# The first block's attention pair by pair of heads, and the first block six weight steps ahead of the second

## The chip, the cores and the metric

The kernel runs on one core of a Trainium2 chip. Its engines run side by side, each with its own instruction queue: TensorE (PE) multiplies, VectorE (DVE), ScalarE (ACT) and GpSimd (POOL) work elementwise, and SyncE (SP) issues most of the data transfers. The time is the device time of one execution in microseconds, and the figure compared is the median of several.

## The reference

Three layers follow each other: a linear attention, a dense feed-forward layer, and a layer with eight experts of which each token takes one.

```python
kv  = einsum('bhsd,bhse->bhde', k, v)          # 4 batches, 8 heads, 576 tokens, 64 columns
out = einsum('bhsd,bhde->bhse', q, kv)
x   = out / sqrt(mean(out*out, -1) + 1e-6) * g_norm      # then [2304, 512]
g   = maximum(x @ w_in, 0) ** 2                # w_in [512, 2048]
x   = g @ w_out                                # w_out [2048, 512]
e   = argmax(x @ w_gate);  gate = softmax(x @ w_gate)[e]  # 8 experts, capacity 576
out = gate * (maximum(x @ w1[e], 0) @ w2[e])   # w1[e] [512, 1024], w2[e] [1024, 512]
```

## The kernel before

**Blocks and units.** The 2304 tokens are six blocks of 384 (`BT`), each of three tiles of 128. A block goes through attention, then through the feed-forward layer, whose 2048 hidden columns are cut into 16 weight steps f of 128. One block at one step is a unit (j, f): `mm1` (L268) is the first product and its squared rectifier, `mm2` (L288) the second product, two units later (`LAG`). All products in full precision are split in a high and a low part and done in three passes (`PASSES`), so each operand needs both parts.

**Weights of the feed-forward layer.** A step's two matrices, w_in and w_out, arrive as 64-bit numbers (`load_m` L142, two transfers of 512 KB a step). `cvt_m` (L151) turns them into 32-bit numbers: ScalarE rescales the upper half (L168), VectorE masks (L169), shifts (L170) and merges (L174). `split_m` (L179) lets ScalarE cast the high part (L183) and GpSimd subtract the low part (L184). In the loop over units, unit (0, f) converts step f + 2 and loads step f + 3.

**Attention of a block.** Heads go in four pairs, so that two heads fill 128 rows. `kv` (L206) multiplies keys and values of one pair and copies the two diagonal blocks to `kvb`, one on ScalarE, one on VectorE. `attn_out` (L217) takes one tile of tokens through all four pairs; ScalarE squares (L236), VectorE sums (L238), GpSimd scales and takes the power -0.5 (L240, L242). `attn_mul` (L244) multiplies on VectorE, and `attn_tr` (L251) transposes on TensorE, with the high part scaled on ScalarE (L259) and the low part on VectorE (L260) into `xT`.

**Order of the work.** The loop over units at the end of the listing writes the program, but a scheduler that works with estimated costs reorders TensorE, VectorE, ScalarE and GpSimd inside a block marked `manual_schedule(engines={SP})`; only SP's queue stays as written. `LEAD = 4` (L525): the first four units are block 0 alone, then units of block 0 and block 1 alternate, so that one converted weight serves both. The second block's attention (`kv_pieces(1)`, `attn_pieces(1)`) is spread over units 0 to 3 (L647). Fills of the scratch and output arrays with zeros (`zeros`) are spread over the units between (1, 2) and (0, 15).

```python
for p in range(NPAIR): kv(0, p)              # L565
for t in range(TB):    attn_out(t)           # L567
for t in range(TB):    attn_mul(t); attn_tr(t)
for f in range(2):     cvt_m(f); split_m(f, wpool)
```

**Buffers.** The pool `wpool` has 24 places of 4 KB a partition. Keys, values and queries of the first two blocks, the staged weights and the split weights of the first 12 steps share them, so a load waits until an earlier tile of its place has been used. The products go to eight banks of PSUM, `pk`: units use pk[0] and pk[1], block 0's results pk[2] to pk[4], and the attention of the front the banks pk[5] to pk[7] in turn (`misc`).

Of the kernel before, what the change touches and what calls it, by code (L numbers as in the profile page):

```python
# [7 lines left out]
F32 = mybir.dt.float32  # L8
F32R = mybir.dt.float32r
# [10 lines left out]
P = 128  # L20
# [6 lines left out]
def attn_moe_kernel(ctx: ExitStack, tc: tile.TileContext, cap, kp, vp, qt, gn, wm, wg, wgt, w1, w2, ident, tri, out):  # L27
# [123 lines left out]
    def cvt_m(f):  # L151


        ws = [stg.pop(("m", f, i)).bitcast(I32).rearrange("p (n t) -> p n t", t=2) for i in range(2)]
        if f < 12:
            h = wpool2.tile([P, 2, 512], F32, tag="w", name="ch")
            o = wpool2.tile([P, 2, 512], F32, tag="w", name="cf")
            parts = [(h, o, slice(0, 2))]
            cvt[f] = [o[:, i, :] for i in range(2)]
        else:  # L160
            hs = [(apool1, apool)[i].tile([P, 1, 512], F32, tag="qx"[i], name="ch") for i in range(2)]
            os = [(apool, apool1)[i].tile([P, 1, 512], F32, tag="kv"[i], name="cf") for i in range(2)]
            parts = [(hs[i], os[i], slice(i, i + 1)) for i in range(2)]
            cvt[f] = [o[:, 0, :] for o in os]
        for h, o, sl in parts:
            hi, oi = h.bitcast(I32), o.bitcast(I32)
            for n, w in enumerate(ws[sl]):
                nc.scalar.activation(out=h[:, n, :], in_=w[:, :, 1].bitcast(F32), func=AF.Copy, scale=2.0 ** -112)  # L168
            nc.vector.tensor_scalar(oi, hi, -(1 << 31), None, op0=ALU.bitwise_and)  # L169
            nc.vector.scalar_tensor_tensor(  # L170
                out=oi, in0=hi, scalar=3, in1=oi, op0=ALU.logical_shift_left, op1=ALU.bitwise_or
            )
            for n, w in enumerate(ws[sl]):
                nc.vector.scalar_tensor_tensor(  # L174
                    out=oi[:, n, :], in0=w[:, :, 0], scalar=29, in1=oi[:, n, :],
                    op0=ALU.logical_shift_right, op1=ALU.bitwise_or,
                )

    def split_m(f, pool):  # L179
        os = cvt.pop(f)  # L180
        for o, d in zip(os, (wi, wo)):
            w = d[f] = pool.tile([P, 2, 512], F32R, tag="w", name="w")
            nc.scalar.copy(w[:, 0, :], o)  # L183
# [22 lines left out]
    def kv(b, p):  # L206
        k, v = kt.pop((b, p)), vt.pop((b, p))
        ps = misc()
        for c in range(NCH):
            nc.tensor.matmul(ps[:, :P], lhsT=k[:, c, :], rhs=v[:, c, :], start=c == 0, stop=c == NCH - 1)  # L210
# [52 lines left out]
        )  # L263


    gt = {}

    def mm1(s):  # L268
        j, f = units[s]
        h = pk[s % 2][:, :BT]  # L270
        n = 0
        for c in range(KD):
            for a, m in PASSES:
                nc.tensor.matmul(  # L274
                    h, lhsT=wi[f][:, a, c * P:(c + 1) * P], rhs=xT[j][:, m, c, :],
                    start=n == 0, stop=n == 3 * KD - 1,
                )
# [244 lines left out]
        d[e, 2 * h], d[e, 2 * h + 1] = split_w(k, engs, pair_tiles(k))  # L522
        ahead(4)

    LAG, LEAD = 2, 4  # L525
    HOT = 9
    MIDDLE = 416
    units = []

    with tc.manual_schedule(engines={mybir.EngineType.SP}):  # L530

        cold = gpool.tile([P, BT], F32, tag="rr", name="cold", bufs=2)[:, :P]
        nc.vector.memset(cold, 0.0)
# [13 lines left out]
        for p in range(NPAIR):
            load_kv(0, p)
            if p == 0:
                nc.sync.dma_start(out=id_sb, in_=ident)  # L550
                nc.sync.dma_start(out=gn_sb, in_=gn)
# [6 lines left out]
        load_m(2)
        load_kv(1, 2)
        load_kv(1, 3)  # L560
        nc.sync.dma_start(out=wg_raw, in_=wg)
        nc.sync.dma_start(out=tri_sb, in_=tri)
        for t in range(TB, 2 * TB):
            load_q(t)
        for p in range(NPAIR):  # L565
            kv(0, p)
        for t in range(TB):  # L567
            attn_out(t)
        for t in range(TB):
            attn_mul(t)  # L570
            attn_tr(t)
        for f in range(2):
            cvt_m(f)
            split_m(f, wpool)
# [501 lines left out]
```

## Time and profile before

| | us |
|---|---|
| median of 3 runs | 759.19 (756.44 to 760.04) |
| the profiled execution | 755.1 |
| its span, first to last instruction | 753.2 |
| TensorE busy | 715.7 (95%) |
| VectorE busy | 371.6 (49%) |
| ScalarE busy | 309.5 (41%) |
| GpSimd busy | 292.3 (39%) |

The shares are means over stages that differ. By 40 slices of the span (18.8 us each), TensorE's busy tenths begin 6 6 7 8 and are then 9 (90% or more) until the last two; VectorE's begin 2 9 8 9 8 6 6. Matmuls are pipelined and their ends modelled. A weight load (PEld) runs beside the matmul before it. "Idle before" is time in which the engine had nothing running ahead of the instruction, with what ended it behind the arrow.

### The profile page before, as it was taken

The numbers are of one execution on the slowest core, as the hardware profiler recorded it, in microseconds if no ns is written. First come the engines' busy times: TensorE is split into PE (matmuls) and PEld (weight loads), VectorE is DVE, ScalarE is ACT, GpSimd is POOL, SyncE is SP. The second block draws the span as 40 slices with busy tenths as digits, with TensorE's granted clock in tenths as the row PEclk, the third lists the DMA queues.
The fourth block names the chain that finished last, engine by engine and source line by source line (L and its number), as shares of the span: only waits on it lengthen the run. The fifth ranks groups of instructions, "written<-read, shape, count | busy, mean of one in ns | idle before, by whom it ended". The sixth has DMA issues, their size and how long they took to land. (4 is left out here: it accounts for less than half of the span.)

```text
span 753.2 us, 12061 instructions
## 1 busy us (share of the span) xinstructions
PE 715.7 (95%) x4012; PEld 637.5 (85%) x4012; DVE 371.6 (49%) x833; ACT 309.5 (41%) x650; POOL 292.3 (39%) x288
## 2 busy tenths in 40 slices
PE   6678999999999999999999999999999999999985
PEld 6667999898899989989898988897888898889764
DVE  2989866548982594349634973331043221133011
ACT  2455454323222332233233264244276544376362
POOL 2566333112022200220130089043469746386881
PEclk9899999999999999999999999999999999999999
DMA  9946798401032202210010176043537554456530
GB/s 326 378 169 201 264 364 293 150 15 67 1 112 87 67 1 70 88 29 0 15 57 1 49 241 204 26 150 121 171 102 219 199 170 148 149 188 212 180 129 19
DMA packets 38016, 102.36 MB, mean 136 GB/s; under 512 B 4451, under 2 KB 4707, under 8 KB 37920
## 3 DMA queue, kind: packets, MB, share of 16 engines
q1 hardware_dynamic: 34912, 91.99, 36.4%
q0 software_dynamic: 3008, 9.10, 3.2%
q8 instruction: 59, 0.97, 0.5%
q14 instruction: 37, 0.30, 0.1%
HBM read 77.78 MB, written 23.91 MB: 135 GB/s over the span
## 5 line engine op out<-in xcount | busy, mean ns | idle before, releaser
L274 PE MATMUL pk<-xT,w 128*128 128x384 f32 x1152 | 223.1, 341 | 8.5 <-POOL w L184 4.6
L293 PE MATMUL pk<-w,g 128*128 128x512 f32 x864 | 218.4, 394 | 2.5 <-ACT g L285 2.5
L274 PEld LDWEIGHTS pk<-xT,w 128*128 128x128 f32 x1152 | 201.5, 188 | 18.6 <-POOL w L184 5.8
L195 POOL TENSOR_TENSOR w<-st,w 128x512 fp32r<-128x512 f32 x128 | 161.5, 1295 | 83.1 <-ACT w L191 83.0
L293 PEld LDWEIGHTS pk<-w,g 128*128 128x128 f32 x864 | 160.2, 188 | 31.7 <-ACT g L285 3.1
L282 ACT ACTIVATE rr<-pk 128x384 f32<-128x384 f32 x96 | 47.1, 492 | 153.6 <-PE pk L274 153.4
L817 PE MATMUL hb<-x,w 128*128 128x256 f32 (+2 forms) x672 | 96.7, 303 | 0.3
L817 PEld LDWEIGHTS hb<-x,w 128*128 128x128 f32 x672 | 93.8, 189 | 1.1 <-issue 0.2
L284 DVE TENSOR_TENSOR pk<-pk,rr 128x384 f32<-128x384 f32 x96 | 54.0, 563 | 74.6 <-ACT rr L282 73.7
L871 DVE SCALAR_TENSOR_TENSOR g<-hb,g 128x576 fp32r<-128x576 f32 (+3 forms) x72 | 40.5, 585 | 97.5 <-ACT g L870 96.5
L103 POOL DMA_INDIRECT disp<-y,sli x18 | 19.1, 1059 | 173.0 <-DVE sli L410 52.9
L355 DVE SCALAR_TENSOR_TENSOR junk<-y,wgb 128x512 f32<-128x512 f32 x120 | 78.0, 684 | 0.7 <-ACT y L313 0.6
L191 ACT CAST w<-st 128x512 fp32r<-128x512 f32 x128 | 71.7, 620 | 13.8 <-DMA st<-in_w 13.4
L285 ACT CAST g<-pk 128x384 fp32r<-128x384 f32 x96 | 46.0, 480 | 72.6 <-DVE pk L284 71.0
L286 DVE TENSOR_TENSOR g<-pk,g 128x384 fp32r<-128x384 f32 x96 | 53.3, 556 | 36.7 <-ACT g L285 36.0
L184 POOL TENSOR_TENSOR w<-cf,w 128x512 fp32r<-128x512 f32 x32 | 47.3, 1494 | 60.9 <-ACT w L183 56.3
L903 PE MATMUL hb<-w,g 128*128 128x512 f32 x264 | 65.7, 407 | 3.1 <-DVE g L871 2.5
L903 PEld LDWEIGHTS hb<-w,g 128*128 128x128 f32 x264 | 50.0, 193 | 15.7 <-DVE g L871 3.4
L870 ACT ACTIVATE g<-hb 128x576 fp32r (+3 forms) x72 | 34.9, 513 | 33.9 <-PE hb L817 29.2
L103 POOL DMA_INDIRECT out<-o,meta x22 | 21.3, 970 | 42.0 <-ACT o L911 17.8
L919 DVE SCALAR_TENSOR_TENSOR o<-bk,meta,o 64x512 f32<-64x512 f32 x3 | 2.3, 752 | 69.5 <-ACT o L918 51.0
L240 POOL TENSOR_SCALAR ms<-ss 128x8 f32<-128x8 f32 x18 | 4.6, 254 | 77.6 <-DVE ss L238 77.3
(138 smaller groups left out, 648.8 us busy)
## 6 DMA issues: line engine op xcount, KB each, us to landing
st<-in_w SPq DMA_DIRECT2D x64, 512.0 KB
st<-in_wm SPq DMA_DIRECT2D x32, 512.0 KB
disp<-zrow SPq DMA_DIRECT2D x9, 1028.0 KB
xr<-disp SPq DMA_DIRECT2D x32, 257.0 KB
k<-in_kp SPq DMA_DIRECT2D x16, 320.0 KB
v<-in_vp SPq DMA_DIRECT2D x16, 320.0 KB
q<-in_qt SPq DMA_DIRECT2D x18, 256.0 KB
out<-zrow SPq DMA_DIRECT2D x9, 512.0 KB
```

Source lines behind the costliest of these rows:

```text
L184: nc.gpsimd.tensor_tensor(w[:, 1, :], o, f32(w[:, 0, :]), op=ALU.subtract)
L191: nc.scalar.copy(w[:, 0, :], s[:, i, :])
L195: e.tensor_tensor(w[:, 1, :], s[:, i, :], f32(w[:, 0, :]), op=ALU.subtract)
L274: nc.tensor.matmul(h, lhsT=wi[f][:, a, c * P:(c + 1) * P], rhs=xT[j][:, m, c, :], start=n == 0, stop=n == 3 * KD - 1,)
L282: nc.scalar.activation(out=r, in_=h, func=AF.Relu)
L284: nc.vector.tensor_tensor(h, h, r, op=ALU.mult)
L285: nc.scalar.copy(g[:, 0, :], h)
L286: nc.vector.tensor_tensor(g[:, 1, :], h, f32(g[:, 0, :]), op=ALU.subtract)
L293: nc.tensor.matmul(ysets[j == 1][i], lhsT=g[:, a, i * P:(i + 1) * P], rhs=wo[f][:, m, :], start=f == 0 and n == 0, stop=f == NF - 1 and n ...
L355: nc.vector.scalar_tensor_tensor(out=junk, in0=yt[j * TB + i][:, :DM], scalar=1.0, in1=wgb[e // 2][:, e % 2, :], op0=ALU.mult, op1=ALU.mul ...
L817: nc.tensor.matmul(h, lhsT=w1_at(e, f // 2, a, c)[:, f % 2 * P:(f % 2 + 1) * P], rhs=x[:, m, c, o:o + w], start=k == 0, stop=k == 3 * KD - 1,)
L903: nc.tensor.matmul(ps[:k, :], lhsT=lhs(f, a), rhs=we2[e, f][:, b, :], start=n == 0, stop=n == len(passes) * NF2 - 1,)
```

## The change

The first block's attention is written pair by pair, and in a block in which no engine is reordered (`manual_schedule()`). Four new functions handle one pair for all three tiles: `first_out`, `first_red`, `first_mul`, `first_tr`, and `first_low` for the low part. They have 384 columns in place of 512, and use six banks in turn. The queries are loaded behind pair 0's keys. The conversion of step 0 is cut in two halves, one for each matrix, and stands among the last pairs; that of step 1 follows behind. `in_order` makes the conversions' rescaling wait for its turn behind the first block (`marks`), and the products of the second block's keys stand behind unit 2. `LEAD` goes from 4 to 6, and the second block's attention is spread over units 2 to 5. Its last two pairs of keys and its queries are loaded behind the weights of steps 3 and 4.

```diff
@@ cvt_m, split_m
-            parts = [(h, o, slice(0, 2))]
+            parts = [(h[:, a:a + n], o[:, a:a + n], slice(a, a + n)) for a, n in (((0, 1), (1, 1)) if f == 0 else ((0, 2),))]
...
+        return [lambda part=part: cvt_part(ws, *part) for part in parts]
+    def cvt_part(ws, h, o, sl):
+        for n, w in enumerate(ws[sl]):
+            a = nc.scalar.activation(out=h[:, n, :], in_=w[:, :, 1].bitcast(F32), func=AF.Copy, scale=2.0 ** -112)
+            if "cvt" in marks:
+                in_order(a, marks["cvt"])
...
@@ kv
+            if "kv" in marks:
+                in_order(a, marks["kv"])
...
+    def first_out(p):
+        ps = ops[p] = misc()
+        for t in range(TB):
+            nc.tensor.matmul(
+                ps[:, t * P:(t + 1) * P], lhsT=qtt[t][:, p, :], rhs=kvb[0][:, p, :],
+                start=t == 0, stop=t == TB - 1, skip_group_check=True,
+            )
...
+        nc.scalar.activation(out=x, in_=ps[:, :BT], func=AF.Square)
+    def first_red(p):
+        nc.vector.tensor_reduce(out=ss, in_=x.rearrange("p (h e) -> p h e", e=DH), axis=AX.X, op=ALU.add)
+        nc.gpsimd.tensor_scalar(ms, ss, 1.0 / DH, 1e-6, op0=ALU.mult, op1=ALU.add)
+        nc.gpsimd.tensor_tensor(r, ms, expo[:, :2 * TB], op=ALU.pow)
...
+    def first_tr(p):
+        for t in range(TB):
+            nc.tensor.transpose(ps[:, t * P:(t + 1) * P], x[:, t * P:(t + 1) * P], id_sb)
+        marks["first"] = nc.scalar.activation(out=d[:, 0, p, :], in_=ps[:, :BT], func=AF.Copy, scale=gn_sb)
...
@@ mm1
+        if s == 2:
+            marks["kv"] = a
...
-    LAG, LEAD = 2, 4
+    LAG, LEAD = 2, 6
-    with tc.manual_schedule(engines={mybir.EngineType.SP}):
+    with tc.manual_schedule():
...
+        load_kv(0, 0)
+        for t in range(TB):
+            load_q(t)
+        load_kv(0, 1)
+        load_kv(0, 2)
+        load_kv(0, 3)
+        load_m(0)
+        load_m(1)
+        load_m(2)
+        load_kv(1, 0)
+        load_kv(1, 1)
+        free[:] = pk[2:8]
+        kv(0, 0)
+        first_out(0)
+        first_red(0)
+        first_mul(0)
+        first_tr(0)
+        kv(0, 1)
+        first_low(0)
+        first_out(1)
+        first_red(1)
+        kv(0, 2)
+        first_out(2)
+        first_mul(1)
+        first_red(2)
+        first_tr(1)
+        kv(0, 3)
+        first_low(1)
+        first_out(3)
+        first_mul(2)
+        first_red(3)
+        first_tr(2)
+        first_low(2)
+        c_in, c_out = cvt_m(0)
+        c_in()
+        split_m(0, wpool, (0,))
+        first_mul(3)
+        first_tr(3)
+        first_low(3)
+        c_out()
+        split_m(0, wpool, (1,))
...
+    with tc.manual_schedule(engines={mybir.EngineType.SP}):
+        marks["cvt"] = marks["first"]
+        for c in cvt_m(1):
+            c()
+        split_m(1, wpool)
...
-        put(0, LEAD, kv_pieces(1) + attn_pieces(1))
+        put(2, LEAD - 2, kv_pieces(1) + attn_pieces(1))
...
+                if s == 0:
+                    load_kv(1, 2)
+                    load_kv(1, 3)
+                if s == 1:
+                    for t in range(TB, 2 * TB):
+                        load_q(t)
```

**TensorE, the front.** Before, from the first pair's product on (v, k are values and keys, kvb the diagonal blocks, q the queries, id_sb the transpositions):

```order
L210 MATMUL pk_93<-v,k 128x128 x5
L210 MATMUL pk_94<-v,k 128x128 x5
L210 MATMUL pk_95<-v,k 128x128 x5
L210 MATMUL pk_93<-v,k 128x128 x5
L228 MATMUL pk_94<-kvb_128,q 128x128 x4
L228 MATMUL pk_95<-kvb_128,q 128x128 x4
L228 MATMUL pk_93<-kvb_128,q 128x128 x4
L255 MATMUL pk_94<-id_sb,x 128x128 x4
L255 MATMUL pk_95<-id_sb,x 128x128 x4
L255 MATMUL pk_93<-id_sb,x 128x128 x4
L210 MATMUL pk_94<-v,k 128x128 x5
L210 MATMUL pk_95<-v,k 128x128 x5
```

Now, from the same place:

```order
L224 MATMUL pk_90<-v,k 128x128 x5
L286 MATMUL pk_91<-kvb_128,q 128x128 x3
L314 MATMUL pk_92<-id_sb,x 128x128 x3
L224 MATMUL pk_93<-v,k 128x128 x5
L286 MATMUL pk_94<-kvb_128,q 128x128 x3
L224 MATMUL pk_95<-v,k 128x128 x5
L286 MATMUL pk_90<-kvb_128,q 128x128 x3
L314 MATMUL pk_91<-id_sb,x 128x128 x3
L224 MATMUL pk_92<-v,k 128x128 x5
L286 MATMUL pk_93<-kvb_128,q 128x128 x3
L314 MATMUL pk_94<-id_sb,x 128x128 x3
L314 MATMUL pk_95<-id_sb,x 128x128 x3
```

A pair's outputs and transpositions now stand ahead of the next pair's product; the second block's keys (pk_94 in the last two rows before) are no longer here but behind the third unit.

**VectorE, the front.** Before, from the sums of the first block's rows on (ss the sums, cf the converted weights, ch their rescaled halves):

```order
L238 TENSOR_REDUCE ss<-x 128x8 x2
L246 TENSOR_TENSOR x<-pk_94,r 128x512
L238 TENSOR_REDUCE ss<-x 128x8
L246 TENSOR_TENSOR x<-pk_95,r 128x512
L169 TENSOR_SCALAR cf<-ch 128x1024
L260 SCALAR_TENSOR_TENSOR xT<-pk_94,gn_sb,xT 128x4x128
L260 SCALAR_TENSOR_TENSOR xT<-pk_95,gn_sb,xT 128x4x128
L246 TENSOR_TENSOR x<-pk_93,r 128x512
L170 SCALAR_TENSOR_TENSOR cf<-ch,cf 128x1024
L169 TENSOR_SCALAR cf<-ch 128x1024
L260 SCALAR_TENSOR_TENSOR xT<-pk_93,gn_sb,xT 128x4x128
L174 SCALAR_TENSOR_TENSOR cf<-st_176,cf 128x512
```

Now, from the last pairs on, with L183, L184 and L188 for the three steps of a conversion:

```order
L229 COPY kvb_128<-pk_92 64x64
L321 SCALAR_TENSOR_TENSOR xT<-pk_91,gn_sb,xT 128x384
L305 TENSOR_TENSOR x<-pk_90,r 128x384
L297 TENSOR_REDUCE ss<-x 128x6
L321 SCALAR_TENSOR_TENSOR xT<-pk_94,gn_sb,xT 128x384
L183 TENSOR_SCALAR cf<-ch 128x512
L184 SCALAR_TENSOR_TENSOR cf<-ch,cf 128x512
L188 SCALAR_TENSOR_TENSOR cf<-st_176,cf 128x512
L305 TENSOR_TENSOR x<-pk_93,r 128x384
L321 SCALAR_TENSOR_TENSOR xT<-pk_95,gn_sb,xT 128x384
L183 TENSOR_SCALAR cf<-ch 128x512
L184 SCALAR_TENSOR_TENSOR cf<-ch,cf 128x512
```

The first conversion, which stood among the first rows' scaling, now stands behind three of the four pairs and its second half behind all.

**ScalarE, between steps.** Before, around the rescaling of steps 5 and 6 (rr, g: a unit's first product; w: a cast weight):

```order
L282 ACTIVATE rr<-pk_89 128x384
L168 ACTIVATE ch<-st_456 128x512
L183 CAST w<-cf 128x512 x2
L168 ACTIVATE ch<-st_458 128x512
L285 CAST g<-pk_89 128x384
L259 ACTIVATE xT<-pk_93,gn_sb 128x4x128
L282 ACTIVATE rr<-pk_88 128x384
L168 ACTIVATE ch<-st_538 128x512
L168 ACTIVATE ch<-st_540 128x512
L183 CAST w<-cf 128x512 x2
```

Now, around the rescaling of steps 5 and 6:

```order
L180 ACTIVATE ch<-st_432 128x512
L347 CAST g<-pk_89 128x384
L197 CAST w<-cf 128x512 x2
L180 ACTIVATE ch<-st_434 128x512
L252 ACTIVATE x<-pk_94 128x512
L344 ACTIVATE rr<-pk_88 128x384
L180 ACTIVATE ch<-st_498 128x512
L347 CAST g<-pk_88 128x384
L252 ACTIVATE x<-pk_95 128x512
L197 CAST w<-cf 128x512 x2
L180 ACTIVATE ch<-st_500 128x512
```

Step 6's rescaling (before: st_538 and st_540, now: st_498 and st_500) stood ahead of the casts of step 5 with both halves; now its second half stands behind them.

## Rows read from the trace of the kernel before

**Rows 1.** Busy us by stretch: PE, PEld, DVE, ACT, POOL; granted clock, DMA share, GB/s.
```profile
0.00:10.00 10.00, 7.13 (x39) 6.81 (x40) 1.92 (x9) 1.70 (x3) 0.51 (x7) 1.00 0.80 252
10.00:20.00 10.00, 6.01 (x48) 5.37 (x48) 3.83 (x8) 3.99 (x8) 4.38 (x6) 0.97 1.04 407
20.00:30.00 10.00, 7.57 (x46) 6.91 (x47) 8.93 (x13) 4.99 (x11) 2.42 (x5) 0.69 1.04 391
30.00:80.00 50.00, 41.23 (x221) 35.39 (x220) 45.69 (x57) 27.44 (x54) 33.89 (x23) 1.00 0.65 225
80.00:160.00 80.00, 80.00 (x403) 72.46 (x402) 48.62 (x76) 33.98 (x67) 20.80 (x18) 1.00 0.68 233
```

**Rows 2.** Timeline, TensorE, 0 to 60: start, us, instructions [idle before].
```profile
7.70 1.35 PE L210 MATMUL pk<-v,k 128*128 128x128 f32 x10 [1.02 <-DMA v<-in_vp]
...
11.44 1.35 PE L210 MATMUL pk<-v,k 128*128 128x128 f32 x10 [0.24 <-DMA v<-in_vp]
12.63 3.00 PE L228 MATMUL pk<-kvb,q 128*128 128x128 f32 x24
18.11 0.63 PE L255 MATMUL pk<-id_sb,x 128*128 128x128 f32 x4 [2.49 <-DVE x L246]
20.12 1.08 PE L255 MATMUL pk<-id_sb,x 128*128 128x128 f32 x4 [1.38 <-DVE x L246]
...
24.34 5.30 PE L210 MATMUL pk<-v,k 128*128 128x128 f32 x36
```

**Rows 3.** Timeline, VectorE, 0 to 60 us.
```profile
13.07 0.23 DVE L213 COPY kvb<-pk 64x64 f32<-64x64 f32 x1 [1.37 <-ACT kvb L212]
...
23.23 1.21 DVE L170 SCALAR_TENSOR_TENSOR cf<-ch,cf 128x1024 int32<-128x1024 int32 x1
24.36 0.68 DVE L169 TENSOR_SCALAR cf<-ch 128x1024 int32<-128x1024 int32 x1
25.30 0.75 DVE L260 SCALAR_TENSOR_TENSOR xT<-pk,gn_sb,xT 128x512 fp32r<-128x512 f32 x1 [0.26 <-ACT xT L259]
25.97 1.28 DVE L174 SCALAR_TENSOR_TENSOR cf<-st,cf 128x512 int32<-128x512 int32 x2
...
28.68 1.29 DVE L174 SCALAR_TENSOR_TENSOR cf<-st,cf 128x512 int32<-128x512 int32 x2
...
30.27 1.40 DVE L169 TENSOR_SCALAR cf<-ch 128x1024 int32<-128x1024 int32 x1
...
33.94 3.34 DVE L174 SCALAR_TENSOR_TENSOR cf<-st,cf 128x512 int32<-128x512 int32 x2
```

**Rows 4.** Timeline, TensorE, 60 to 80 us.
```profile
71.28 1.66 PE L293 MATMUL pk<-w,g 128*128 128x512 f32 x6 [2.47 <-ACT g L285]
...
75.58 2.28 PE L274 MATMUL pk<-xT,w 128*128 128x384 f32 x12
```

**Rows 5.** Timeline, VectorE, 60 to 80 us.
```profile
73.37 1.63 DVE L169 TENSOR_SCALAR cf<-ch 128x1024 int32<-128x1024 int32 x1
```

**Rows 6.** Timeline, GpSimd, 0 to 60 us.
```profile
15.56 1.68 POOL L242 TENSOR_TENSOR r<-ms,expo 128x8 f32<-128x8 f32 x1
...
29.73 9.91 POOL L184 TENSOR_TENSOR w<-cf,w 128x512 fp32r<-128x512 f32 x6 [7.51 <-ACT w L183]
```

**Rows 7.** Busy time of a short stretch.
```profile
20.00:22.00 2.00, 1.08 (x4) 0.71 (x4) 1.27 (x3) 0.76 (x2) 1.93 (x3) 0.50 1.05 409
```

**Rows 8.** Timeline, ScalarE, 0 to 60 us.
```profile
58.03 1.24 ACT L168 ACTIVATE ch<-st 128x512 f32<-128x512 f32 x2
59.38 1.23 ACT L183 CAST w<-cf 128x512 fp32r<-128x512 f32 x2
```

**Rows 9.** Groups by line, VectorE, 30 to 80 us: busy, mean ns, idle before.
```profile
L170 DVE SCALAR_TENSOR_TENSOR cf<-ch,cf 128x1024 int32<-128x1024 int32 x7 | 13.4, 1919 | 0.1
L174 DVE SCALAR_TENSOR_TENSOR cf<-st,cf 128x512 int32<-128x512 int32 x14 | 11.6, 857 | 0.0
L169 DVE TENSOR_SCALAR cf<-ch 128x1024 int32<-128x1024 int32 x7 | 7.4, 1056 | 0.8 <-ACT ch L168 0.6
```

More of the change, by code (lines that the diff above doesn't have):

```diff
@@ L118, in after_scatters, with in_order @@
             )
+    def in_order(later, first):
+        later, first = getattr(later, "ins", later), getattr(first, "ins", first)
+        tc.add_manual_dep(
+            later, first.name, mybir.DependencyInfo(mybir.DependencyClass.NoSync, mybir.DependencyReason.SCHED_ONLY),
+            reason="the order in which the loads come in",
+        )
+    marks = {}
     kt, vt, qtt = {}, {}, {}
@@ L164, in cvt_m, with split_m @@
             cvt[f] = [o[:, 0, :] for o in os]
[L165 to L169, printed above, removed]
+        return [lambda part=part: cvt_part(ws, *part) for part in parts]
+    def cvt_part(ws, h, o, sl):
+        hi, oi = h.bitcast(I32), o.bitcast(I32)
+        for n, w in enumerate(ws[sl]):
+            a = nc.scalar.activation(out=h[:, n, :], in_=w[:, :, 1].bitcast(F32), func=AF.Copy, scale=2.0 ** -112)
+            if "cvt" in marks:
+                in_order(a, marks["cvt"])
+        nc.vector.tensor_scalar(oi, hi, -(1 << 31), None, op0=ALU.bitwise_and)
+        nc.vector.scalar_tensor_tensor(
+            out=oi, in0=hi, scalar=3, in1=oi, op0=ALU.logical_shift_left, op1=ALU.bitwise_or
+        )
+        for n, w in enumerate(ws[sl]):
             nc.vector.scalar_tensor_tensor(
-                out=oi, in0=hi, scalar=3, in1=oi, op0=ALU.logical_shift_left, op1=ALU.bitwise_or
-            )
[L173 to L183, printed above, removed]
+                out=oi[:, n, :], in0=w[:, :, 0], scalar=29, in1=oi[:, n, :],
+                op0=ALU.logical_shift_right, op1=ALU.bitwise_or,
+            )
+    def split_m(f, pool, which=(0, 1)):
+        for i in which:
+            o = cvt[f][i]
+            w = (wi, wo)[i][f] = pool.tile([P, 2, 512], F32R, tag="w", name="w")
+            marks["split"] = nc.scalar.copy(w[:, 0, :], o)
             nc.gpsimd.tensor_tensor(w[:, 1, :], o, f32(w[:, 0, :]), op=ALU.subtract)
@@ L209, in kv @@
         for c in range(NCH):
-            nc.tensor.matmul(ps[:, :P], lhsT=k[:, c, :], rhs=v[:, c, :], start=c == 0, stop=c == NCH - 1)
+            a = nc.tensor.matmul(ps[:, :P], lhsT=k[:, c, :], rhs=v[:, c, :], start=c == 0, stop=c == NCH - 1)
+            if "kv" in marks:
+                in_order(a, marks["kv"])
         d = kvb[b % 2]
@@ L273, in mm1 @@
             for a, m in PASSES:
-                nc.tensor.matmul(
+                a = nc.tensor.matmul(
                     h, lhsT=wi[f][:, a, c * P:(c + 1) * P], rhs=xT[j][:, m, c, :],
@@ L545, in attn_moe_kernel @@
         nc.vector.tensor_copy(base, ecap_i)
[L547 to L551, printed above, removed]
+        load_kv(0, 0)
+        nc.sync.dma_start(out=id_sb, in_=ident)
+        nc.sync.dma_start(out=gn_sb, in_=gn)
         for t in range(TB):
             load_q(t)
+        load_kv(0, 1)
+        load_kv(0, 2)
+        load_kv(0, 3)
         load_m(0)
         load_m(1)
+        load_m(2)
+        nc.sync.dma_start(out=wg_raw, in_=wg)
+        nc.sync.dma_start(out=tri_sb, in_=tri)
         load_kv(1, 0)
         load_kv(1, 1)
[L558 to L566, printed above, removed]
-        for t in range(TB):
[L568 to L574, printed above, removed]
+        free[:] = pk[2:8]
[28 more added lines that the diff above has]
+        split_m(0, wpool, (1,))
+        for t in range(TB):
+            qtt.pop(t)
+        free[:] = ysets[1]
+    with tc.manual_schedule(engines={mybir.EngineType.SP}):
[3 more added lines that the diff above has]
+        split_m(1, wpool)
+        marks["cvt"] = marks["split"]
         done_b = [1]
@@ L683, in attn_moe_kernel @@
                 load_m(f + 3)
+                if s == 0:
[4 more added lines that the diff above has]
+                        load_q(t)
             if j == 0 and f + 2 < NF:
-                cvt_m(f + 2)
+                for c in cvt_m(f + 2):
+                    c()
+                marks.pop("cvt", None)
                 split_m(f + 2, wpool if f + 2 < 12 else wpool2)
@@ L695, in attn_moe_kernel @@
                 p_()
+            if s == LEAD:
+                marks.pop("kv", None)
             fl = s - at[NB - 1, 0]
```

22 lines of the change are left out of this document (added).

## The prediction

> **What bounds the kernel now.** The first view is the busy time by stretch [rows 1]. From 80 us on TensorE is busy 80.00 of 80.00, so nothing at the front can shorten what follows; it can only let that saturated part start sooner or later. All that can move is TensorE's idle time ahead of 80: 2.87 + 3.99 + 2.43 in the first three tens and 8.77 in 30 to 80, 18.1 in all, with some work at the lower clock. In the same rows VectorE is busy 8.93 of 10 from 20 to 30 and 45.69 of 50 from 30 to 80, so VectorE sets the pace from 20 on and is mostly free before that (1.92 and 3.83 of 10).
>
> The second view is TensorE's timeline at the start [rows 2]. The four products of keys and values run as their data land (7.70, 11.44), the outputs at 12.63, and then TensorE waits three times for VectorE's scaled rows (18.11, 20.12 and the next). The second block's keys (24.34, 5.30 us) fill a gap in which the weights were not ready. The third view is VectorE's timeline [rows 3]: the weight conversion (three steps: mask, shift, merge) of step f=0 is spread through the attention of the first block, f=1's ends at 28.68 + 1.29 = 29.97, and f=2's runs from 30.27 to 33.94 + 3.34 = 37.28. The last view is the stretch from 60 to 80 [rows 4, 5]: TensorE's last real stall is the 2.47 us ahead of 71.28, for squared rows that VectorE had not got to.
>
> So the question is when VectorE has done a given amount of work. I take a mark that is comparable in both programs: the first conversion step of f=8, at 73.37 before [rows 5]. In the old order the conversions of f=0 to 7, the rows g of seven units and both attentions stand ahead of it. In the new order the same stands ahead, but for two short instructions. The six-step lead therefore neither adds to nor takes from VectorE's work up to the mark, and behind it both programs give TensorE two units per weight. The mark's shift is VectorE's extra idle time plus the change in what collisions cost it.
>
> **Term A: the first block pair by pair.** The new TensorE order is: pair 0's product, its outputs, its transpositions, and only then pair 1's product; two more such rounds follow, for pair 1 (with pair 2 inside it) and pair 3. One round, from first output product to last transposition, took 12.63 to 18.11 + 0.63 = 18.74, that is 6.11 us [rows 2], of which the power on GpSimd is 1.68 [rows 6]. A pair has three quarters of the columns of a token tile; taking a quarter off what is neither the power nor hand-overs (about 3.5 us) gives 5.3. Between rounds stand a product of 1.35 [rows 2] and the copies of its two diagonal blocks, which ended 13.07 + 0.23 = 13.30 for a product that ended 12.79, so 0.5 [rows 2, 3].
>
> Start: the queries now come where pair 1's keys and values did (7.70), with 0.13 MB more, so at about 8.1; two thirds of the output products are done by then, which puts the round's start at 7.6. Then 7.6 + 5.3 = 12.9; + 1.85 + 5.3 = 20.05; + 1.85 + 5.3 = 27.2; half a microsecond for pair 3's scaling, which now stands on VectorE behind the conversion of f=0's first matrix: 27.7 is the end of the last transposition, against about 24.3 before, where the next products begin. [...]
>
> [...]
>
> Behind the last transposition ScalarE scales it (0.5), then starts f=0's second matrix (0.62) and f=1's two (1.24) [rows 8]; VectorE needs 0.68, 1.21 and 1.28 for a whole conversion [rows 3] and half of that for one matrix. Following VectorE's new order, f=1's conversion ends 6.8 us after the last transposition, at 34.5 to 36.2 against 29.97. The instructions ahead of that point differ by about half a microsecond in either direction (one g more, two copies fewer). A is +4.5 to +6.2; if the power shrinks with the six columns it now has instead of eight, 0.4 less in each of three rounds, +3.3. I take +5.4.
>
> **Term B: fewer collisions.** f=2's conversion took 7.01 us for 3.17 us of own work while GpSimd ran six subtractions without a break (9.91 us) [rows 3, 6]. Over 30 to 80 seven conversions took 13.4 + 11.6 + 7.4 = 32.4 us instead of 22.2 [rows 9]. Without f=2's 3.8 the other six lost (10.2 - 3.8) / 6 = 1.1 each. In the new order f=0's and f=1's subtractions come one by one, so f=2 should lose what the others do: B is -2.7, between 0 and -3.8.
>
> [...]
>
> **Term C: the second block ends later.** Its last transposed rows (0.75 [rows 3]) now stand behind the mark, with one g and the mark itself, about 2.3 us. The first unit of block 1 needs them. TensorE's state there corresponds to 75.58 less one unit (2.28) = 73.3 before [rows 4], practically the mark; it can do five products in the meantime, about 1 us. C is +1.0, between 0 and +2.3.
>
> **Term D: ScalarE's order.** In the new order the second rescaling of f=4, 5, 6 and 8 stands behind both casts of the step before it; in the old one only f=5's does, and f=7's and f=8's behind one. VectorE's next mask waits casts 1.23 plus 0.62 [rows 8] behind its last merge, of which g's two steps cover about 1.1: 0.7 a time, two or three times more often. D is +1.5, between 0 and +3.
>
> **What I cost at nothing.** The second block's keys lose their free gap (5.30 us at 24.34 [rows 2]); they now stand behind three units, where TensorE waits for VectorE anyway (8.77 us idle from 30 to 80 [rows 1]). Without that cover they cost up to 5.3. Data: by 30 us the queue moved 2.5 + 4.1 + 3.9 = 10.5 MB [rows 1]; in the new order of loads the second block's last keys end at 10.4 MB, ahead of their use at about 45. The staging of f=6 and 7 now waits for the second block's keys to be used, and SP's queue waits behind it; that comes some 5 us before their conversion. The 18 fills with zeros are spread over 13 steps instead of 17 and stand behind f=11's weights; the queue was 0.68 busy from 80 to 160 [rows 1], so they find room; a late f=14 or 15 would cost a few microseconds.
>
> **The sum.** 5.4 - 2.7 + 1.0 + 1.5 = +5.2. The profiled execution took 755.1 (span 753.2 and 1.9 around it), so 760.3 for the like. The median of the runs, 759.2, lies 4.1 above that execution, and on it the forecast is 764.4.
>
> **Rivals.**
> - Given back in the lead (no change). VectorE idles 4.3 us in 30 to 80 already [rows 1], the power is short, the clock holds, f=2 meets no subtraction: 3.3 - 3.8 + 1.0 + 0.5 = +1.0, 760. For it: A's price rests on a chain of waits, and B is large in the trace. Against it: D and C point the other way.
> - Faster: the second block's deadline is the bound. It moves from step 5 to step 7, and the 2.47 us at 71.28 and the waits for weights in 30 to 80, 8.77 together, are the price of squeezing its attention into four steps [rows 1, 4]. If all of that vanished, and C's microsecond with it: 5.4 - 8.8 - 1.0 = -4.4, 754.8. Against it: VectorE, not the order, fills that stretch, and its work up to the mark is the same. It decides if f=1's weights are ready by about 32.
> [...]
>
> **Chances.** The forecast has 0.46 (its own range 761 to 769, nearly all above the bound), no change 0.24, faster 0.20, slower by more 0.10. A measurement of this kernel can tell about 0.5% from no change, 3.8 us. Faster 0.20, same 0.27, slower 0.53. The two ends of the four terms are -0.5 and +11.5; with half of the faster case and most of the slower one the range is 754 to 771.
>
> **What would show it.** Right: three rounds of 5 to 5.5 us each on TensorE, the first conversion of f=1 ending near 35, f=2's conversion shorter than 7 us, the mark at 76 to 80, TensorE full soon after, and the part behind it unchanged. A is wrong if the last transposition comes before 26; B if f=2 still takes 7 us; D if VectorE hardly waits for ScalarE from 40 on. The whole is wrong if TensorE is full before 75, or if waits turn up behind 90 us.

## The result and the profile after

The changed kernel took 765.99 us (median of 4 runs, 764.24 to 767.47), the kernel before beside it 757.82 (4 runs, 754.86 to 760.04). The ratio is 1.0115 [1.0084, 1.0147]: slower, by 8.2 us. Measured again beside the kernel before (e8), it was 766.85 against 756.19, 1.0128 [1.0102, 1.0154]. The profiled execution took 766.68 (span 764.7).

The busy time by stretch of the changed kernel, to be held against [rows 1]:

```profile
0.00:10.00 10.00, 7.20 (x34) 6.50 (x34) 1.54 (x8) 1.56 (x3) 0.50 (x7) 0.97 0.75 248
10.00:20.00 10.00, 5.45 (x32) 4.99 (x33) 2.73 (x6) 1.90 (x5) 2.34 (x4) 0.68 1.03 411
20.00:30.00 10.00, 4.72 (x32) 3.92 (x31) 5.71 (x11) 3.62 (x8) 5.45 (x9) 0.83 1.04 393
30.00:80.00 50.00, 42.82 (x218) 34.60 (x216) 41.49 (x57) 27.47 (x55) 26.76 (x21) 0.93 0.43 140
80.00:160.00 80.00, 78.35 (x394) 70.65 (x395) 54.07 (x82) 36.72 (x72) 26.63 (x20) 1.00 0.81 286
```

From 20 to 30 us VectorE, which set the pace before (8.93), is busy 5.71; and TensorE does less in those ten us (4.72 for 7.57). Behind its last stall (88.88) TensorE is full, as it was before behind 71.28 [rows 4]. The count of products in the units (keys and attention left out) that the timeline has before 110 us tells what that is worth: 169 of the first and 108 of the second kind, where the kernel before had 197 and 126. At 2.28 us for 12 and 2.24 for 9 that is 5.3 + 4.5 = 9.8 us of work not yet done. The two profiled executions differ by 11.5 us in span, so most of that is lost by 110 us.

TensorE's timeline at the start, the rounds, for [rows 2] (start, us, instructions, idle before):

```profile
7.38 0.80 PE L286 MATMUL pk<-kvb,q 128*128 128x128 f32 x4 [0.56 <-DVE kvb L229]
9.27 0.62 PE L286 MATMUL pk<-kvb,q 128*128 128x128 f32 x2 [1.09 <-DMA q<-in_qt]
13.44 0.87 PE L314 MATMUL pk<-id_sb,x 128*128 128x128 f32 x3 [3.55 <-issue]
14.11 2.34 PE L224 MATMUL pk<-v,k 128*128 128x128 f32 x10
17.00 0.94 PE L286 MATMUL pk<-kvb,q 128*128 128x128 f32 x6 [0.56 <-DVE kvb L229]
...
21.40 0.55 PE L314 MATMUL pk<-id_sb,x 128*128 128x128 f32 x3 [0.86 <-DMA tri_sb<-in_tri]
...
23.63 0.94 PE L286 MATMUL pk<-kvb,q 128*128 128x128 f32 x6 [0.56 <-DVE kvb L229]
24.74 0.55 PE L314 MATMUL pk<-id_sb,x 128*128 128x128 f32 x3 [0.18 <-DVE x L305]
28.98 0.87 PE L314 MATMUL pk<-id_sb,x 128*128 128x128 f32 x3 [3.69 <-DVE x L305]
29.51 4.27 PE L334 MATMUL pk<-xT,w 128*128 128x384 f32 x12
```

The rounds took 6.9 (from 7.38), 4.95 (17.00 to 21.95) and 6.2 us (23.63 to 29.85). The first holds a wait for the last queries (1.09). The first unit took 4.27 us for 12 products where it took 2.39 before:

```profile
31.16 2.39 PE L274 MATMUL pk<-xT,w 128*128 128x384 f32 x12 [0.63 <-POOL w L184]
```

The granted clock was 1.00 there (30 to 34 us), and 0.50 in the changed kernel (28 to 32):

```profile
10.00:16.00 6.00, 2.56 (x12) 0.50 1.04 413
...
18.00:26.00 8.00, 5.14 (x38) 1.00 1.04 394
...
28.00:32.00 4.00, 3.02 (x10) 0.50 1.04 405
...
38.00:40.00 2.00, 2.00 (x7) 0.50 0.33 123
```

These are stretches of the same kernel (TensorE's busy time, granted clock, DMA share, GB/s): in three the granted clock is 0.50, and with them go idle times of 3.55, 3.69 and 1.93 us (ahead of 13.44, 28.98 and 35.71).

VectorE's timeline, for [rows 3, 5]: the conversion of f=1 (mask, shift, merge), the first step of f=2, and the mark:

```profile
32.24 0.69 DVE L183 TENSOR_SCALAR cf<-ch 128x1024 int32<-128x1024 int32 x1
...
33.45 1.22 DVE L184 SCALAR_TENSOR_TENSOR cf<-ch,cf 128x1024 int32<-128x1024 int32 x1
...
35.05 2.25 DVE L188 SCALAR_TENSOR_TENSOR cf<-st,cf 128x512 int32<-128x512 int32 x2
...
39.13 1.38 DVE L183 TENSOR_SCALAR cf<-ch 128x1024 int32<-128x1024 int32 x1 [1.35 <-ACT ch L180]
...
42.48 1.29 DVE L188 SCALAR_TENSOR_TENSOR cf<-st,cf 128x512 int32<-128x512 int32 x2
...
80.70 0.69 DVE L183 TENSOR_SCALAR cf<-ch 128x1024 int32<-128x1024 int32 x1 [0.21 <-ACT ch L180]
```

f=1's conversion ends at 37.30 (29.97 before), and the mark stands at 80.70 (73.37): both 7.33 us later. What VectorE waited for between 28 and 82 us (us in all, times, longest):

```profile
DVE cf L183 <- ACT ch L180: 3.8, 5, 1.3
DVE x L262 <- POOL r L258: 3.2, 1, 3.2
DVE xT L321 <- ACT xT L316: 1.7, 1, 1.7
...
```

Between 20 and 75 before, the first kind of wait came to 0.6 in one, the second to 1.8 in two. TensorE's last stall, for [rows 4], stands behind the mark now:

```profile
88.88 1.66 PE L355 MATMUL pk<-w,g 128*128 128x512 f32 x6 [1.21 <-ACT g L347]
```

It waits for g, and on VectorE g waits behind f=9's shift, where two units' multiplications come together:

```profile
85.62 2.22 DVE L184 SCALAR_TENSOR_TENSOR cf<-ch,cf 128x1024 int32<-128x1024 int32 x1
87.76 1.02 DVE L346 TENSOR_TENSOR pk<-pk,rr 128x384 f32<-128x384 f32 x2
```

### The profile page after: what moved, and what is told of

It is laid out like the page before. It is cut to its first block, busy times and chain, and to the rows that moved or that the text cites. A ratio compares the mean times of both kernels' runs of the same rounds, so it can differ in the third digit from the quotient of the medians.

```text
span 764.7 us, 12075 instructions
## 1 busy us (share of the span) xinstructions
PE 723.1 (95%) x4012; PEld 640.6 (84%) x4012; DVE 369.9 (48%) x838; ACT 310.7 (41%) x652; POOL 292.3 (38%) x290
## 4 chain that ended last, share of the span: by engine, by line
PE 67%; DMA 13%; DVE 7%; POOL 4%; issue 4%; ACT 3%; SPq 0%; POOLq 0%; ACTq 0%; DVEq 0%
PE pk L334 22%; PE pk L355 22%; DMA out<-o,meta 9%; PE hb L916 8%; PE hb L1002 6%; PE bk L1002 4%; POOL w L209 2%; PE pk L224 1%; PE pk L244 1%; DVE cf L184 1%; DVE g L970 1%; POOL r L258 1%; POOL w L198 1%; ACT w L205 1%; DVE junk L417 1%
## 5 line engine op out<-in xcount | busy, mean ns | idle before, releaser
L334 PE MATMUL pk<-xT,w 128*128 128x384 f32 x1152 | 226.6, 344 | 5.5 <-POOL w L198 2.1
L334 PEld LDWEIGHTS pk<-xT,w 128*128 128x128 f32 x1152 | 203.6, 190 | 17.5 <-POOL w L198 4.7
L1002 PE MATMUL bk<-w,g 128*128 128x512 f32 x120 | 28.6, 396 | 0.0
```

The costliest lines, as they stand in the source:

```text
L334: a = nc.tensor.matmul(h, lhsT=wi[f][:, a, c * P:(c + 1) * P], rhs=xT[j][:, m, c, :], start=n == 0, stop=n == 3 * KD - 1,)
L1002: nc.tensor.matmul(ps[:k, :], lhsT=lhs(f, a), rhs=we2[e, f][:, b, :], start=n == 0, stop=n == len(passes) * NF2 - 1,)
```

## The experiments

Two ideas stood against each other. Rounds: a round of product, power and scaling costs time for each pair, so f=1's conversion and all behind it come later. Keys and lead: taking the second block's keys out of TensorE's gap costs, by idle time, by the clock or by the lead of six. Each ratio is against the kernel before measured beside it (754.89 us for e1 to e4, 756.19 for e5 to e8, 757.43 for e9 to e12). The starts are those of the last of the first block's transpositions, of f=1's and f=8's masks (the mark) on VectorE, and of TensorE's work behind its last stall. The last column is the units' work not done by 110 us, counted as above, in us against the kernel before.

| run | median us | ratio [95%] | last transp. | f=1 | mark | last stall | less by 110 |
|---|---|---|---|---|---|---|---|
| before | | | 23.46 | 24.36 | 73.37 | 71.28 |  |
| changed | 765.99 | 1.0115 [1.0084, 1.0147] | 28.98 | 32.24 | 80.70 | 88.88 | 9.8 |
| e1 lead and loads alone | 760.56 | 1.0075 [1.0055, 1.0096] | 23.89 | 24.79 | 74.42 | 84.72 | 5.3 |
| e2 pairs alone | 762.52 | 1.0107 [1.0085, 1.0129] | 28.28 | 36.19 | 84.13 | 73.10 | 6.7 |
| e3 rounds overlapped | 763.22 | 1.0102 [1.0078, 1.0126] | 26.72 | 29.96 | 78.74 | 86.90 | 7.7 |
| e4 gaps filled | 765.65 | 1.0139 [1.0114, 1.0164] | 27.91 | 30.77 | 77.86 | 88.26 | 10.7 |
| e5 lead six only | 757.36 | 1.0013 [0.9996, 1.0030] | 23.22 | 24.12 | 76.28 | 75.61 | 2.2 |
| e6 as e1, filled, 36 | 766.70 | 1.0119 [1.0093, 1.0146] | 25.56 | 26.46 | 77.08 | 87.37 | 8.3 |
| e7 f=0 converted early | 764.61 | 1.0101 [1.0072, 1.0129] | 29.90 | 33.07 | 79.92 | 88.08 | 9.0 |
| e8 changed again | 766.85 | 1.0128 [1.0102, 1.0154] | 28.79 | 32.02 | 80.55 | 88.72 | 9.6 |
| e9 lead six, keys late | 762.21 | 1.0062 [1.0042, 1.0082] | 23.66 | 24.57 | 73.88 | 85.19 | 5.3 |
| e10 as e1, filled, 18 | 766.88 | 1.0121 [1.0087, 1.0155] | 23.11 | 24.01 | 75.25 | 85.62 | 8.1 |
| e11 e3 and e7 together | 763.56 | 1.0076 [1.0048, 1.0104] | 27.80 | 30.65 | 79.25 | 87.42 | 8.3 |
| e12 e11, keys early | 763.67 | 1.0076 [1.0048, 1.0103] | 27.82 | 34.24 | 82.89 | 81.89 | 7.5 |

In every run the work not done by 110 us lies within 2.3 us of what the median lost; the mark and the last stall do not even put the runs in order (e2 loses 7.6 us with its last stall at 73.10).

**The two halves.** e1 keeps the old first block and takes the new lead, the loads and the rule on the keys; e2 the reverse, with the second block's loads where they were.

```diff
 e1
-        kv(0, 0); first_out(0); first_red(0); first_mul(0); first_tr(0) ...
+        for p in range(NPAIR): kv(0, p)
+        for t in range(TB): attn_out(t)
+        for t in range(TB): attn_mul(t); attn_tr(t)
 e2
-    LAG, LEAD = 2, 6
+    LAG, LEAD = 2, 4
-        put(2, LEAD - 2, kv_pieces(1) + attn_pieces(1))
+        put(0, LEAD, kv_pieces(1) + attn_pieces(1))
```

> The first block's attention as before (tile by tile, reordered by the scheduler, conversions of steps 0 and 1 free to fill gaps), with the rest of the change: lead of six, the second block's keys behind three units, its last loads behind the weights of steps 3 and 4. Theory 1 (the rounds of the first block delay VectorE's first conversions): the mark at 73 to 76, only the terms C and D are left, 760 us. Theory 2 (the lead and the late keys cost the time): about as slow as the changed kernel, 765.

> The first block pair by pair as in the changed kernel, with the lead of four, the second block's loads and keys as before the change. Theory 1: the last transposition still near 29.9 and f=1's conversion still ending near 37, so 763 to 766. Theory 2: near the kernel before, 758.

Both halves cost by themselves, +5.7 and +7.6 us, and together not the 13.3 of the sum but 8 to 11. In numbers e1 came out on theory 1's line and e2 half a microsecond under it; that e1's price is that of the terms C and D is not shown, and e5 and e9 below speak for the keys. e2's price is not that of the rounds alone: the second block's keys stand ahead of the first unit there (28.95, 4.88 us), and f=1's mask came 4 us later than in the changed kernel. The pairs are better priced by taking them out of the whole, which is e1: 1.0075 for 1.0115 and 1.0128, so 0.4 to 0.5%, clear of the intervals in the second case only. TensorE in e1 behind the third transposition, where the kernel before had keys (24.34, 5.30 us [rows 2]):

```profile
23.89 1.09 PE L271 MATMUL pk<-id_sb,x 128*128 128x128 f32 x4 [2.25 <-DVE x L262]
27.79 1.01 PE L334 MATMUL pk<-xT,w 128*128 128x384 f32 x2 [2.81 <-ACT w L197]
29.99 4.21 PE L334 MATMUL pk<-xT,w 128*128 128x384 f32 x12 [1.20 <-POOL w L198]
35.09 3.57 PE L334 MATMUL pk<-xT,w 128*128 128x384 f32 x10 [0.89 <-POOL w L198]
```

The gap stayed empty, and the first two units ran at a granted clock of 0.50 (20 to 36 us). The mark moved by 1.05 only; the price of e1 lies where the mark doesn't show it.

**Rounds overlapped (e3).** Pair 1's products ahead of pair 0's scaling:

```diff
         first_red(0)
-        first_mul(0)
-        first_tr(0)
         kv(0, 1)
-        first_low(0)
         first_out(1)
+        first_mul(0)
         first_red(1)
+        first_tr(0)
+        first_low(0)
```

> The changed kernel with one move: pair 1's keys and outputs stand ahead of pair 0's scaling and transpositions, so the first round overlaps the second. Theory 1: the last transposition 3 to 4 us earlier, at 26, f=1's conversion and the mark as much earlier, 762 to 763. Theory 2: no change, 766.

```profile
26.72 0.88 PE L314 MATMUL pk<-id_sb,x 128*128 128x128 f32 x3 [3.69 <-DVE x L305]
...
86.90 1.43 PE L355 MATMUL pk<-w,g 128*128 128x512 f32 x5 [1.22 <-ACT g L347]
```

TensorE in e3: the last transposition is 2.26 us sooner, the last stall 1.98; the mark is 1.96 sooner. So a shift in the rounds goes through to the end of the paced stretch nearly one for one. By 110 us e3 has done 2.1 us more than the changed kernel. The medians differ by 2.8 us, but were not measured side by side, and the ratios overlap.

**Gaps filled in the changed kernel (e4).** Products of constants that nobody reads, 22 in the first gap and 16 in the last:

```diff
         first_out(0)
+        for i in range(22):
+            nc.tensor.matmul(pk[0][:, :P], lhsT=cold, rhs=cold, start=True, stop=True)
         first_red(0)
...
         first_tr(2)
+        for i in range(16):
+            nc.tensor.matmul(pk[0][:, :P], lhsT=cold, rhs=cold, start=True, stop=True)
```

> The changed kernel with 38 products of zeros added in two gaps of TensorE (22 behind pair 0's outputs, 16 behind pair 2's transpositions), into a bank that the first unit overwrites. If the low clock carries a good part of term A: no stretch at 0.50 from 10 to 40, first unit 2.4 us instead of 4.3, mark and time 2 to 3 us earlier, 763 to 764. If VectorE's order alone sets the mark: the clock is up and the time is the same, 766.

The clock was 1.00 to 30 us and the first unit ran as fast as before, and then:

```profile
29.35 2.03 PE L334 MATMUL pk<-xT,w 128*128 128x384 f32 x10 [0.57 <-POOL w L198]
34.24 0.79 PE L355 MATMUL pk<-w,g 128*128 128x512 f32 x1 [2.86 <-ACT g L347]
...
36.94 3.57 PE L334 MATMUL pk<-xT,w 128*128 128x384 f32 x10 [0.36 <-POOL w L198]
```

The time won was given back as a wait for g (2.86 us), behind which the clock fell again: 0.70 from 30 to 40 us, and ten products took 3.57. The mark came 2.84 us sooner, as the first idea had it, and the time did not: 765.65. A faster clock up to 30 us was worth nothing that could be measured. The clock is not all that differs, though: the scheduler set VectorE's and ScalarE's order otherwise from the second unit on (its multiplication stands behind f=2's merges, ahead of them in the changed kernel).

**The lead alone (e5) and the keys alone (e9).** e5 is one number in the kernel before; e9 adds the rule that holds the keys behind three units, and with it spreads the second block's attention over units 2 to 5.

```diff
 e5, e9
-    LAG, LEAD = 2, 4
+    LAG, LEAD = 2, 6
 e9
+            if "kv" in marks:
+                in_order(a, marks["kv"])
+        if s == 2:
+            marks["kv"] = a
-        put(0, LEAD, kv_pieces(1) + attn_pieces(1))
+        put(2, LEAD - 2, kv_pieces(1) + attn_pieces(1))
```

> The kernel before with the first block's lead raised from four to six and nothing else: first block, load order and the second block's attention from the first step on are as before, so the second block's keys stay in TensorE's gap at 24 to 29 us. Theory L (the lead itself costs): VectorE paces until step f=8 and TensorE has two second-block units (2 x 4.2 us) less to do by then, of which it gets back what VectorE saves on those units' steps; last stall of TensorE near 85 us instead of 71.28, as in the run with the new lead and loads, clock of 20:30 near 0.69 as before, time 758 to 761. [...]

> The kernel before with a lead of six and, beside it, only the rule that the second block's keys stand behind three of the first block's units; first block and loads as before. With the lead alone the time was 757.36 (1.0013 of before), with lead, loads and this rule 760.56 (1.0075). [...] Rival (the price is the later loads of the second block, which the rule only follows): first units near 2.39 us, 756.5 to 758.

The lead alone is within measurement of nothing; with the keys held back it costs 0.62%, most of what e1 lost (0.75%). For a free lead and a price on the keys alone, the author's forecast was within 0.2% of the kernel before in e5, and 760 to 761.5 us in e9; in the ratios (1.0013, 1.0062) it holds in both, and theory L and the loads fall. Whether the keys cost by the low clock (0.53 from 20 to 30 us in e9, 0.66 in e5) or by another thing, the two runs do not tell. TensorE in e5, then in e9:

```profile
24.10 5.96 PE L210 MATMUL pk<-v,k 128*128 128x128 f32 x36
...
31.91 2.38 PE L274 MATMUL pk<-xT,w 128*128 128x384 f32 x12 [0.74 <-POOL w L184]
...
37.83 0.71 PE L293 MATMUL pk<-w,g 128*128 128x512 f32 x2
...
79.75 2.22 PE L293 MATMUL pk<-w,g 128*128 128x512 f32 x9
```

```profile
27.56 1.01 PE L285 MATMUL pk<-xT,w 128*128 128x384 f32 x2 [2.81 <-ACT w L192]
29.77 6.12 PE L285 MATMUL pk<-xT,w 128*128 128x384 f32 x22 [1.19 <-POOL w L193]
39.45 0.73 PE L306 MATMUL pk<-w,g 128*128 128x512 f32 x2 [3.56 <-ACT g L298]
...
45.40 3.51 PE L219 MATMUL pk<-v,k 128*128 128x128 f32 x30
...
84.18 0.73 PE L306 MATMUL pk<-w,g 128*128 128x512 f32 x2 [0.55 <-ACT g L298]
```

In e5 the keys fill the gap, and there is no stall behind the two units at 75.61. In e9 the same products take 3.51 us and 1.27 (at 52.95) between units, 22 products of the first two units take 6.12 us at a granted clock of 0.53 (20 to 30 us) and 0.79 (30 to 40), where e5 did 12 in 2.38 at 1.00 (30 to 40), and TensorE waits 3.56 for the first g, since ScalarE has the casts of f=2 ahead of the unit's Relu and they wait for VectorE:

```profile
36.62 1.27 ACT L192 CAST w<-cf 128x512 fp32r<-128x512 f32 x2 [4.01 <-DVE cf L183]
37.80 0.48 ACT L295 ACTIVATE rr<-pk 128x384 f32<-128x384 f32 x1
```

e9's mark is 2.4 us sooner than e5's and its time 0.5% longer: the mark says when VectorE has converted, not how much TensorE has done.

**e1 with its gap filled (e6, e10).**

```diff
+        for i in range(18):
+            a = nc.tensor.matmul(pk[0][:, :P], lhsT=cold, rhs=cold, start=True, stop=True)
+            in_order(a, marks["tr"])
```

> The run with the old first block, the new lead and the new loads, plus 36 products of constants (128x128) behind the third transposition, where the kernel before has the second block's first 36 products of keys (24.34, 5.30 us); their results are not used. It takes away the low clock and leaves the order of all other work. Theory K (what that kernel loses, 5.7 us, is mostly the low clock of its first two units, about 4 us read from 4.21 for 2.39 and 3.57 for 2.03 and the products behind them): 756 to 757.5. Theory L (VectorE paces to the mark, so units that end sooner only wait longer; the loss is that TensorE has less to do before the mark): 759.5 to 761, with the units at 2.03 to 2.4 us and the time saved coming back as idle time before 70 us.

> Old first block, new lead, new loads, with 18 products of constants in the gap behind the third transposition: half as many as in the filled run before, where 36 products left 72 records and held TensorE until 36.6 us. 18 leave 36 records, as many as the second block's keys left there in the kernel before (24.34, 5.30 us). Theory K1 (the price of the moved keys is the clock of the first units): first two units at 2.0 to 2.4 us, 756 to 758. Theory K2 (the price is the key products themselves, which filled a free gap and now take 5.3 us of TensorE's time between units): units as fast, but the time stays at 759 to 761, the gain coming back as idle time before 70 us.

e6 was a miss in size: its products held TensorE for 10.39 us, and the first unit began at 36.59. In e10 they took 5.97:

```profile
23.99 5.97 PE L631 MATMUL pk<-cold 128*128 128x128 f32 x36
29.71 3.03 PE L334 MATMUL pk<-xT,w 128*128 128x384 f32 x14
34.33 3.40 PE L334 MATMUL pk<-xT,w 128*128 128x384 f32 x10 [1.59 <-POOL w L198]
...
85.62 2.83 PE L355 MATMUL pk<-w,g 128*128 128x512 f32 x6 [2.35 <-ACT g L347]
```

Only the first unit got faster; the second waited for GpSimd's subtraction all the same. f=3's mask came at 39.04 (38.87 in e1). The time was 766.88, above what either theory gave, of which rows show 0.9 us at the last stall and about 1.6 at a lower clock behind it (2.83 for 1.65, 2.67 for 2.27; granted 0.83 from 80 to 90 us, 1.00 in e1). K1's time did not come, but K1 is not refuted: the second unit stayed slow, a new low clock was paid for behind 85 us, and the scheduler set ScalarE's and VectorE's order otherwise than in e1 (f=3's mask stands behind the second unit's multiplication, ahead of it in e1). The waits of 3.55, 3.69 and 1.93 us in the changed kernel stand beside a granted clock of 0.50; in no run here did filling a wait with idle products save time that could be measured (e4 765.65 for 765.99, e6 766.70 and e10 766.88 for e1's 760.56).

**f=0 converted early (e7), beside the changed kernel (e8); with the overlap (e11).**

```diff
         first_red(1)
+        c_in, c_out = cvt_m(0)
+        c_in()
...
         first_red(2)
+        c_out()
...
-        c_in, c_out = cvt_m(0)
-        c_in()
...
-        c_out()
```

> The changed kernel with the conversion of step f=0 moved forward: its two halves stand behind the second and third group's sums of squares (near 19 and 24 us), where VectorE is idle for about 3 us in each round, instead of behind the third and fourth low rows (26.49 and 31.07). Nothing else is moved. Theory A (the path runs over the rounds and VectorE's first conversions to the mark): f=1's conversion begins near 30.5 instead of 32.24, the mark comes 1.5 to 2 us sooner (79 instead of 80.70), and the time is 1.5 to 2 us under that of the changed kernel in this same comparison. Rival (ScalarE's casts and GpSimd's subtraction, or the order of the last rounds, pace there): f=1's conversion or the mark moves by under 0.5 us and the time is the changed kernel's within 0.5 us. If the halves delay the multiplications they now stand ahead of, the last transposition ends later than 29.85 and the time is 1 to 2 us more.

> The changed kernel, once more, beside the others of this comparison, so that differences of a few us between its variants are read on one chip: 763.5 to 767, 1.0 to 1.4% over the kernel before, mark near 80.7 and last stall near 88.9 us.

> The changed kernel with both moves that were tried one at a time: the second group's products of keys and queries ahead of the first group's multiplication, and f=0's conversions in VectorE's idle time of the second and third round. Theory A (the path runs over the rounds and VectorE's first conversions to the mark and the last stall): the gains add, f=1's conversion begins near 28.5 us instead of 32.24, mark near 77 instead of 80.70, last stall near 85 to 86.5 instead of 88.88, time 3.5 to 5 us under the changed kernel: 760 to 763. Rival (another chain, ScalarE's casts or GpSimd's subtractions, takes over): no sooner than the run with the first move alone, 763 or more, mark at 78.7 or later.

e7's median is 2.2 us under e8's, as theory A said, but not by its path: f=1's conversion did not come sooner but 1.05 us later, and the mark 0.63 sooner; the intervals overlap, so the gain is not shown. The last transposition ended later than 29.85, the case for which 1 to 2 us more were expected, and they did not come. ScalarE in e7 tells why (us, tile, idle before):

```profile
30.81 0.58 ACT L316 ACTIVATE xT<-pk,gn_sb 128x384 fp32r<-128x384 f32 x1 [2.61 <-PE pk L314]
31.29 0.61 ACT L197 CAST w<-cf 128x512 fp32r<-128x512 f32 x1
31.80 1.24 ACT L180 ACTIVATE ch<-st 128x512 f32<-128x512 f32 x2
```

f=1's rescaling (`ch`) stands behind the last round's copy, by a rule of the change. From the start of the last transposition to f=1's mask it was 3.26 us in the changed kernel, 3.24 in e3, 3.17 in e7, 2.85 in e11. VectorE's own order there does not matter; the last round does. e11 was 3.3 us under the changed kernel's second median in time, but its mark was 79.25 and not 77: that is the rival's line. By the mark and by the work done by 110 us the gains of e3 and e7 don't add; the ratios (1.0102 and 1.0101, together 1.0076, for 1.0128) would let them, with intervals too wide to tell.

**Both moves and early keys (e12).**

> Both moves as in the run with the two together, with the lead of six, but the second block's loads early and its keys free to stand ahead of the first unit, where the pairs alone had them (28.95, 4.88 us). Theory: the late keys' price and the rounds' price are each taken back in part: first unit behind the keys near 32 to 33 us, time 757 to 761, thus not under the kernel before (the third and fourth rounds still end 5 us later than its third transposition, 24.55). Rival (rounds no longer count once conversions are early): 753 to 756. Rival (the keys ahead of the first unit hold it up, as in the run of the pairs alone, 762.5): 762 to 765.

```diff
 e11 and
-        if s == 2:
-            marks["kv"] = a
-        put(2, LEAD - 2, kv_pieces(1) + attn_pieces(1))
+        put(0, LEAD, kv_pieces(1) + attn_pieces(1))
```

The second block's loads stand where e2 has them. At 763.67 it is the last rival's line: the first unit came at 32.49, where the theory had it, but not the time. No version beat the kernel before.

## Why the forecast came out so

- **Term A** had the right mechanism and was mis-sized: f=1's conversion ended 7.33 us later, forecast +5.4 with +6.2 as the end. The rounds were put at 5.3 us each and took 6.9, 4.95 and 6.2. The queries were not all there at 8.1 (the wait ends at 9.27), and the third round, for which half a microsecond of scaling was added, has a wait of 3.69: its power ended at 27.37, and the scaling, behind f=0's first matrix on VectorE, began at 28.29. Behind the last transposition it took 7.45 us for 6.8. The power did shrink, to 1.32 to 1.36 us with six columns, from 1.68 with eight [rows 6]. A's upper end held 1.7 us for one drop of the clock, an estimate of the author's that no run shows. Shown is a granted clock of 0.50 in three stretches of the changed kernel (10 to 16, 28 to 32 and 38 to 40 us), as before from 20 to 22 [rows 7]; in the first, pair 0's transpositions and pair 1's product took 0.87 and 2.34 us, where the same forms took 0.55 and 1.28 at 1.00 (21.40 and 21.79): 1.4 more.
- **Terms B, C and D**: f=1's end and the mark moved by the same 7.33, so B and D, which lie between them, came to 0.0 with all else there, forecast -1.2 (C lies behind the mark). B was right: f=2's conversion took 39.13 to 43.77, 4.64 for 7.01, -2.4. C was small: the second block's last low rows stand at 81.78, behind the mark as said. D was too low: the waits for the rescaling went from 0.6 to 3.8, +3.2 for +1.5. The four steps that it named waited 2.5 us (f=4, 5, 6 and 8), and f=2's mask, which it had not, 1.35. Not foreseen was the second block's scaling behind two subtractions on GpSimd, the one wait of 3.2 us in place of 1.8 in all. Other waits and collisions make up the rest and were not traced one by one.
- **"What I cost at nothing"** did not hold where it could be tested. The second block's keys were to be hidden where TensorE waits for VectorE anyway; with the old first block holding them back costs 0.5% (e9 against e5), some 3.7 us, and the upper end given, 5.3 us, was the better guess. "The six-step lead neither adds nor takes" held for the lead alone (e5). What they cost in the full change is not separated: e2, without late keys, already stands at 1.0107, but pays for them ahead of the first unit.
- **The mark** was a poor measure of the end. It was to come at 76 to 80 and came at 80.70, 3.1 us later than A, B and D gave: A was 1.9 short, B and D 1.2. It told VectorE's time well, but the last stall moved from f=7's step to f=9's, where two units' multiplications stand on VectorE behind the shift. Before, the last stall of 2.47 us stood ahead of the mark; now it ends 8.2 us behind it. The mark's +7.3 became 9.8 us of work not done by 110 us, so 2.5 us were lost elsewhere than at the mark, where C had +1.0. The rise was forecast at 5.2 and measured at 8.2 us, and at 10.7 the second time; 764.4 came within 1.6 of 765.99 in part because the median that it was set on, 759.2, lay 1.4 above the later one.
- Slower by more was put at +12.5 (no gap for the keys, a low clock through the first unit), which no run shows: 8.2 and 10.7 came. Its mechanism was partly right: no gap, and the first unit at a granted clock of 0.50 (28 to 32 us). "Faster" fell at its own point of decision, f=1's weights by about 32.
- What stays open: how the 0.5% of the late keys splits between TensorE's time for them (4.8 us between units), the low clock of the first units (0.53 from 20 to 30 us in e9), and the new order on ScalarE and VectorE that the rule brings about.

## What to carry to other kernels

Where an engine waits for a paced one, work that filled its gap was free there (e5, 1.0013), and not surely elsewhere: moved to "somewhere it also waits", the keys here cost 0.5%, with another order on ScalarE and a stall. A run that adds idle products under a scheduler tests the clock and a new order at once. Cost a chain of small steps round by round, with each hand-over, and look at what stands between its end and the pacing engine: here some 3 us, most of them on ScalarE, lay between the last transposition and f=1's mask. Measure the end by the work that the last engine has done by a given time, not by when one step of another engine begins.

## What had not been expected of the hardware

- Eighteen products of 128x128 in fp32 left 36 records in the trace of e10 and took 5.97 us at a granted clock of 0.69 (24 to 30 us).
- GpSimd's power of 128x6 elements took 1.33 us where 128x8 took 1.68 [rows 6]: a fifth less for a quarter fewer columns.
- VectorE's steps on int32 in SBUF took 1.38 and 2.20 us beside GpSimd's subtractions (39.13 and 44.86), and 0.69 and 1.22 without (32.24 and 33.45), as before; its steps on PSUM took 0.55 and 0.56 beside them (79.94 and 34.59). Not every meeting costs: f=8's mask (80.70) took 0.69 while two subtractions ran (79.55, 3.01).
